# An attention and bilinear-GLU block: the condition and beta arrive as rows, one block of the modulation weights is loaded ahead of x, half of segment 1's row statistics move among the gates, and the first fifteen slots are filled evenly

## The chip, the cores and the metric

One core of a Trainium2 chip runs the whole program. The metric is the device time of one execution in microseconds (us). The kernel before has a median of 853.55 us over three runs (853.47 to 854.69).

## What is computed

`x` has 2048 rows of 512 columns. A condition vector `c` (512 numbers) gives six modulation vectors. The block is an adaptive layer norm, an attention over four segments of 512 rows with a memory carried from segment to segment, and a bilinear GLU. `_layernorm` subtracts the mean of a row and divides by the root of its variance plus 1e-5; `_silu(c)` is c / (1 + exp(-c)).

```python
x = A_x
mod = (_silu(c) @ w_mod).reshape(c.shape[0], 6, 1, -1)
sa, ca, ga, sb, cb, gb = (mod[:, i] for i in range(6))
h = _layernorm(x) * (1 + ca) + sa
x = x + ga * attention(h, wq, wk, wv, wo, beta)
h = _layernorm(x) * (1 + cb) + sb
x = x + gb * (((h @ w_gate) * (h @ w_up)) @ w_down)

# attention: H = 32 heads of 16, N = 4 segments of 512 rows, g = sigmoid(beta) for each head
for s in range(4):
    p = softmax(q_s k_s^T / 4 + mask)        # within the segment
    a_dot = p v_s
    a_mem = phi(q_s) M / (phi(q_s) z + 1e-6)  # phi(t) = t + 1 for t > 0, else exp(t)
    o_s = g * a_mem + (1 - g) * a_dot
    M, z = M + phi(k_s)^T v_s, z + sum(phi(k_s))
return o @ wo
```

The inputs are fp32. The kernel splits fp32 operands into a high and a low part (names that end in H and L) and adds three products.

## The kernel before, in words

The work on TensorE is kept in one written order: each matmul goes through a helper (`MM` and `TP`, L85 and L88) that chains it to the matmul before. Many VectorE and ScalarE instructions of the opening go through such chains too (`CV` and `CA`, L39). The scheduler places other instructions between them; `pin` ties one behind the last TensorE instruction. DMAs of weights and of `x` are issued by the SP queue, in its own order; two small ones by ScalarE's queue.

**The opening.** `s_c` is silu(c), kept as 128 partitions x 4 columns, so that each column scales one block of 128 rows of `w_mod`. `c` comes by a DMA straight into that layout; `beta` comes by a DMA that copies its 32 numbers to all 128 partitions (tile `be`). `xload(0)` issues the four 128x512 tiles of segment 0 of `x`; `wm0_load(j)` issues half j of the shift and scale columns of `w_mod` as four tiles `wm0_k` (k = 0 to 3, 256 KB each). `warm(NWU)` puts 18 matmuls on a tile of zeros (`wu` into `wups`) ahead of all other TensorE work. Then come

- `mod0(0)`: 16 fp32 matmuls (32 records of 128x96 in the profile, tile `m`) that multiply the first half of the columns with `s_c`,
- the 16 transposes of the normalised `x` (tile `atp`),
- `mod0(1)`: the second half. Its first two blocks are added up before, by ScalarE (`wm` scaled by `s_c`) and VectorE (scalar_tensor_tensor on `wm`), so 12 matmuls are left,
- the projections `kps`, `qps`, `vps` of segment 0, from `h` (tiles `ahH`, `ahL`).

VectorE takes the statistics of the four tiles of `x` (`bn_stats` and `bn_aggr`, tiles `ast`, `amv`) and normalises them in `ln`. `mod0_out` copies the modulation to `modc`, which ScalarE needs to build `ahf`.

**The gates.** `gates()` (about 27 to 37 us) makes `gg` = 1 + exp(-beta) and `omg` = 1 + exp(beta) and their reciprocals on VectorE; GpSimd puts `omg` into the `v` tiles and multiplies the masks `hmg`.

**The slots.** After that a loop over units `v` from -2 to 32 runs the attention, five slots a unit. A unit is four heads of one segment. In a slot, `q_half` runs q matmuls into bank `lq0` or `lq1` and a VectorE reduction that finds the row maximum (custom instruction, tiles `q` and `nm`); the bank is free for the next q matmul when the reduction is done. `k_step` runs the k matmuls into bank `lk`, ScalarE takes the exponential (tile `pt`). Between them `fill(share, ...)` takes steps from a generator of side work: it adds `share * 5.5` us of credit in each slot and spends it. The side work of segment 0 is the rest of the projections, the memory (`mp`, `mz`) and segment 1's layer norm (`a_ln(1)`), which the generator `weave` puts between the steps of the last q and k projections. In units -2, -1 and 0 there is no earlier unit to finish (`prev` is false); these are the first fifteen slots.

Of the kernel before, what the change touches and what calls it, by code (L numbers as in the profile page):

```python
# [8 lines left out]
F32 = mybir.dt.float32  # L9
# [8 lines left out]
P = 128  # L18
S, D, H, DH, NSEG, L, F = 2048, 512, 32, 16, 4, 512, 1376
KT = D // P  # L20
# [37 lines left out]
def tile_kernel(ctx, tc, x, wq, wk_, wv, wo, beta, w_gate, w_up, w_down, c, w_mod, out):  # L58
# [113 lines left out]
    def ln(pool, hpool, xt, s, sc, sh, pfx, hb, fast):  # L172
# [4 lines left out]
        for t in range(4):  # L177
            st = pool.tile([P, 6], F32, tag="st", name=f"{pfx}st{s}_{t}", bufs=2)
            i = V.bn_stats(st, xt[t])
            if not first:  # L180
                pin(i)
            V.bn_aggr(mv[:, t, :], st)
            if not first:
                yield 0.0
        sd = pool.tile([P, 4], F32, tag="sd", name=f"{pfx}sd{s}", bufs=2)
# [439 lines left out]

    pwpool, pw = open_pool(name="pw", bufs=1, reuse_waits="tile")
    papool, pa = open_pool(name="pa", bufs=2, reuse_waits="tile")
    nc.scalar.dma_start(s_c, c)
    wm = w_mod.rearrange("(k p) n -> p k n", p=P)

    def load_mod(i):
# [7 lines left out]
    def xload(s):  # L639
# [4 lines left out]
            xt.append(a)  # L644
        return xt

    xts = {0: xload(0)}
    NWU = 18
    wu = pa.tile([P, 512], BF, tag="rl", name="wu", bufs=1)
    vec.memset(wu, 0.0)  # L650
    wups = psp.tile([P, 2, 512], F32, tag="lk", name="wups", bufs=1)
# [2 lines left out]
        for i in range(n):  # L654
            MM(wups[:, 0], wu[:, 0:P], wu, start=True, stop=True)

    warm(NWU)
    wm0 = []
    for k in range(KT):
        a = ap.tile([P, 2, 2, 256], F32, tag="pt", name=f"wm0_{k}", bufs=PT)  # L660
        wm0.append(a)

    def wm0_load(j):
        for k in range(KT):
            pin(nc.sync.dma_start(wm0[k][:, j], wm[:, k, :].rearrange("p (i c) -> p i c", c=D)[:, 0:2, 256 * j:256 * j + 256]))

    wm0_load(0)
    r0 = [[a[:, j].rearrange("p i c -> p (i c)") for a in wm0] for j in range(2)]
    nc.scalar.dma_start(be, beta[None, :].to_broadcast([P, H]))
    act.activation(e1, s_c, AF.Exp, scale=-1.0)  # L670
    CV.tensor_scalar_add(e1, e1, 1.0)
    CV.reciprocal(e1, e1)
    scl = CV.tensor_mul(s_c, s_c, e1)
    for a in kst:
        tc.add_manual_dep(nc.gpsimd.memset(a[96:98].rearrange("p h t -> p (h t)").bitcast(F32), ONES2).ins, scl.ins.name, SYNC, reason="order")

    def gates():

        CA.activation(gg, be, AF.Exp, scale=-1.0)
        act.activation(omg, be, AF.Exp)  # L680
        CV.tensor_scalar(omg, omg, 1e30, 1.0, op0=ALU.min, op1=ALU.add)
        for a in vt[0] + vt[1]:
            nc.gpsimd.tensor_copy(a[:, 0:H * VS].rearrange("p (h e) -> p h e", e=VS)[:, :, DH], omg)
        CV.tensor_scalar_add(gg, gg, 1.0)
        for tl in (gg, omg):
            CV.reciprocal(tl, tl)
        for g in range(NG):
            nc.gpsimd.tensor_mul(hmg[:, g, :, 0:DH], hmg[:, g, :, 0:DH],
                                 gg[:, g * HG:(g + 1) * HG].unsqueeze(2).to_broadcast([P, HG, DH]))
            nc.gpsimd.tensor_mul(hmg[:, g, :, DH], hmg[:, g, :, DH], omg[:, g * HG:(g + 1) * HG])  # L690
# [28 lines left out]
    def mod0(j, ks=range(KT)):  # L719
        ps = mp0[j].rearrange("p (i n) -> p i n", n=P)[:, :, 0:MW]  # L720
        for k in ks:
            f = s_c[:, k:k + 1].to_broadcast([P, MW]) if len(ks) == KT or k > 1 else ones[:, 0:MW]
            for i in range(4):
                MM(ps[:, i], r0[j][k][:, i * P:(i + 1) * P], f,
                   start=k == ks[0] and i == 0, stop=k == KT - 1, skip_group_check=True)

    hcur = [None]

# [13 lines left out]
                i += 1  # L742

    wH, wL = {}, {}
    stage = [("ph", 3), ("ph", 3), ("ph", 3), ("mem", 1), ("pkr", 1), ("f", 2)] + [("x", 4)] * 4 + [("mem", 1), ("memb", 2)]
    nst = [0]

    def staged(nm):
        tg, n = stage[nst[0] % len(stage)]
        nst[0] += 1  # L750
        return (ap if tg == "memb" else pa).tile([P, D], F32, tag=tg, name=f"wr{nm}", bufs=n)

    def load_g(nm, w, g):
# [223 lines left out]
    def fill_a():  # L977
# [1 line left out]
            next(w)  # L979
        yield from av  # L980
        memq.extend((a_mem(0, 0), a_mem(0, 1)))
        lns = None
        for s in range(NSEG):
            if s > 0:
                hcur[0] = yield from lns
# [2 lines left out]
            for g in range(2 if s == 0 else 0, NG):  # L988
# [693 lines left out]
```

## Time and profile before

| | |
|---|---|
| Median of three runs | 853.55 us |
| Profiled execution | 854.15 us |
| Its span in the profile | 852.4 us |
| PE busy | 835.3 us (98%) |
| DVE busy | 643.1 us (75%) |
| ACT busy | 499.0 us (59%) |
| POOL busy | 276.8 us (32%) |

PE is TensorE's matmuls, PEld its weight loads, DVE is VectorE, ACT is ScalarE, POOL is GpSimd. A row of the timeline has the start, the busy time, the engine, the line, the operation, output <- input and the count; brackets give the idle time before it and who ended it. In rows that sum up a stretch (its start and end, its length, then busy time of each engine with its count, the granted clock, the DMA share and GB/s) the busy times are to be held against the length of the stretch. A matmul's busy time is longer than its spacing from the next one, because matmuls overlap; spacing is taken from starts.

### The profile page before, as it was taken

Reading aid. Unit: us, or ns where it says so; the run is one execution under the profiler, and the core shown is the slowest. Engines: PE = TensorE matmul, PEld = TensorE weight load, DVE = VectorE, ACT = ScalarE, POOL = GpSimd, SP = SyncE. Lnnn points to the kernel's source line nnn. Section 1 sums busy time; section 2 is a strip of 40 time slices with the busy share of each in tenths; the row PEclk is TensorE's granted clock in tenths of the full one; section 3 lists DMA queues with packets and bytes.
Section 4 is the critical chain, followed back from the end, with each engine's and each line's share of the span. In section 5 each row is a group of like instructions: output and inputs, shape, how many; then the busy total and the mean of one; then the engine's idle time right before and its main releaser. Section 6 shows DMA issues by size and latency. Waiting matters only on the chain.

```text
span 852.4 us, 14404 instructions
## 1 busy us (share of the span) xinstructions
PE 835.3 (98%) x4972; PEld 597.4 (70%) x4972; DVE 643.1 (75%) x1797; ACT 499.0 (59%) x760; POOL 276.8 (32%) x423
## 2 busy tenths in 40 slices
PE   9989999999999999999999999999999999999998
PEld 6756656666665656666665687888888778888886
DVE  7897768887778967787888359989987855447654
ACT  4758767787676876677545626344435555555330
POOL 2756627566565774675434610000000000000000
PEclk9999999999999999999999999999999999999999
DMA  9645435563545554466675466587650685335102
GB/s 271 155 152 155 121 104 141 158 179 115 143 106 166 144 165 106 122 170 213 195 216 155 145 192 230 189 287 271 253 201 28 234 271 210 121 135 184 43 8 98
DMA packets 83928, 139.57 MB, mean 164 GB/s; under 512 B 12720, under 2 KB 46768, under 8 KB 83856
## 3 DMA queue, kind: packets, MB, share of 16 engines
q1 hardware_dynamic: 83424, 138.51, 52.0%
q8 instruction: 39, 0.64, 0.3%
q14 instruction: 33, 0.27, 0.1%
q10 hardware_dynamic: 432, 0.15, 0.1%
HBM read 89.87 MB, written 48.50 MB: 162 GB/s over the span
## 4 chain that ended last, share of the span: by engine, by line
PE 61%; DVE 5%; ACT 1%; issue 0%; POOL 0%; DVEq 0%
PE acc L1358 14%; PE Xg L1289 7%; PE Xu L1289 6%; PE wops L85 5%; PE tb L85 5%; PE Yu L1289 4%; PE Yg L1289 4%; PE k L85 3%; PE q L85 3%; DVE q L39 2%; PE Zg L1289 1%; PE Zu L1289 1%; PE qps L85 1%; PE vps L85 1%; PE Xx L1289 1%; PE up L85 1%
## 5 line engine op out<-in xcount | busy, mean ns | idle before, releaser
L39 DVE CUSTOM_DVE_ANT_0 q<-q,cmask 128x384 f32<-128x384 f32 (+3 forms) x512 | 248.2, 503 | 71.1 <-PE q L85 63.5
L335 ACT ACTIVATE pt<-k 128x1024 f32<-128x1024 f32 x160 | 164.0, 1025 | 74.2 <-PE k L85 71.4
L341 POOL TENSOR_SCALAR_AFFINE_SELECT pt<-pt 128x256 f32<-128x256 f32 (+1 forms) x224 | 98.0, 452 | 137.2 <-ACT pt L335 136.9
L85 PE MATMUL q<-kst,qst 96*128 96x384 bf16 (+3 forms) x512 | 122.8, 302 | 6.5 <-DVE nm L39 5.1
L85 PE MATMUL k<-qst,kst 98*128 98x384 bf16 (+3 forms) x512 | 96.0, 299 | 1.6 <-ACT pt L335 1.3
L1366 DVE TENSOR_TENSOR xa<-xa,acc 128x512 f32<-128x512 f32 x95 | 64.9, 684 | 39.6 <-PE acc L1358 37.8
L85 PEld LDWEIGHTS <-qst 96*128 96x128 bf16 x512 | 43.9, 98 | 58.4 <-issue 43.6
L85 PE MATMUL tb<-pt,v 128*32 128x512 f32 (+3 forms) x1024 | 75.5, 436 | 0.0
L39 DVE DVE_READ_ACCUMULATOR2_ANT nm<- 128x1 f32 x512 | 71.8, 140 | 0.0
L85 PEld LDWEIGHTS <-kst 98*128 98x128 bf16 x512 | 44.4, 98 | 24.9 <-issue 8.8
L1358 PE MATMUL acc<-dH,mH 128*128 128x512 f32 (+1 forms) x152 | 60.3, 397 | 0.0
L1358 PE MATMUL acc<-dL,mH 128*128 128x512 f32 (+1 forms) x152 | 60.1, 395 | 0.0
L1358 PE MATMUL acc<-dH,mL 128*128 128x512 f32 (+1 forms) x152 | 60.0, 395 | 0.0
L85 PEld LDWEIGHTS tb<-pt,v 128*32 128x32 f32 x1024 | 28.7, 109 | 38.6 <-issue 35.7
L367 ACT ACTIVATE tsb<-tb 128x512 f32<-128x512 f32 x32 | 19.1, 596 | 31.6 <-PE tb L85 31.5
L1358 PEld LDWEIGHTS acc<-dH,mL 128*128 128x128 f32 (+1 forms) x152 | 28.5, 188 | 7.1 <-DVE mL L1309 0.3
L1358 PEld LDWEIGHTS acc<-dL,mH 128*128 128x128 f32 (+1 forms) x152 | 28.6, 188 | 7.0
L1358 PEld LDWEIGHTS acc<-dH,mH 128*128 128x128 f32 (+1 forms) x152 | 28.5, 188 | 6.8
L85 PE MATMUL kps<-ahH,wkH 128*128 128x512 f32 x64 | 29.4, 460 | 0.0
L85 PE MATMUL qps<-ahH,wqH 128*128 128x512 f32 x64 | 28.7, 448 | 0.2 <-DVE oL L39 0.2
L85 PE MATMUL vps<-wvH,ahH 128*128 128x512 f32 x64 | 28.3, 442 | 0.0
L85 PE MATMUL wops<-woH,oH 128*128 128x512 f32 x64 | 28.3, 442 | 0.0
(403 smaller groups left out, 2019.1 us busy)
## 6 DMA issues: line engine op xcount, KB each, us to landing
wm<-in_w_mod_dram SPq DMA_DIRECT2D x24, 256.0 KB, 3.9
kd<-k SPq DMA_DIRECT2D x16, 384.0 KB, 2.5
qd<-q SPq DMA_DIRECT2D x16, 384.0 KB, 3.5
kst<-kd SPq DMA_DIRECT2D x32, 192.0 KB, 3.2
qst<-qd SPq DMA_DIRECT2D x32, 192.0 KB, 3.7
x<-in_x_dram SPq DMA_DIRECT2D x16, 256.0 KB, 4.8
kst<-kd SPq DMA_DIRECT2D x32, 128.0 KB, 3.2
qst<-qd SPq DMA_DIRECT2D x32, 128.0 KB, 3.7
```

The source lines that it names most:

```text
L39: i = getattr(self.eng, name)(*a, **k)
L85: return pe(nc.tensor.matmul(*a, **k))
L335: ex = act.activation(pt, kp, AF.Exp, scale=0.25)
L341: sels[u, i] = nc.gpsimd.affine_select(w, w, pattern=[[0, w.shape[1]], [1, P]], compare_op=ALU.is_ge, fill=0.0, base=0, channel_multiplier=-1)
L367: act.activation(tsbs[u], tbs.pop(u), AF.Copy)
L1289: pe(nc.tensor.matmul(ps[0:n], a, b[:, k], start=first and c == 0, stop=last and c == 5, skip_group_check=True))
L1358: pe(nc.tensor.matmul(ps, a[0:m, t * P:(t + 1) * P], b[0:m], start=j == 0, stop=j == n - 1))
L1366: vec.tensor_add(xa, xa, ps)
```

## The change

It does four things.

1. `c` is loaded as 4 rows of 128 numbers and `beta` as one row of 32, and two small TensorE matmuls (`cps`, `bps`) lay them out over the partitions: `crow` against the identity, and a column of ones against `brow`. ScalarE then takes the exponential from `cps` and copies `bps` to `be`. The last steps of `s_c` on VectorE (`condition()`) stand behind the statistics of the first tile of `x`.
2. SP issues the first of the four `wm0` tiles of half 0 ahead of the four tiles of `x`, the other three behind them. The 18 warm-up matmuls become 3, then `cps` and `bps`, then 2, then block 0 of `mod0(0)`, then 4, then blocks 1 to 3.
3. Segment 1's `x` is issued before the last weight loads of the opening, and the statistics of its first two tiles stand next to the two reciprocals in `gates()`. The third is taken in the slot of the q projection where the first two stood. Four staging buffers of the weights move from the `x` ring to the `pt` ring.
4. In units -2, -1 and 0 the share is 0.2 in each of the five slots, in place of 0.25, 0, 0.25, 0.25, 0.25.

```diff
@@ in ln
             V.bn_aggr(mv[:, t, :], st)
+            if first and t == 0:
+                condition()
@@
-    nc.scalar.dma_start(s_c, c)
+    crow = pa.tile([P, D], F32, tag="mem", name="crow", bufs=1)[0:KT, 0:P]
+    brow = pa.tile([P, D], F32, tag="pkr", name="brow", bufs=1)[0:1, 0:H]
+    nc.scalar.dma_start(crow, c)
+    nc.scalar.dma_start(brow, beta[None, :])
@@
-    xts = {0: xload(0)}
-    NWU = 18
...
-    warm(NWU)
...
-    wm0_load(0)
+    wm0_load(0, (0,))
+    xts = {0: xload(0)}
...
+    warm(3)
+    cps = pst((P, KT), "sm", "cps")
+    MM(cps, crow, ident[0:KT, 0:KT], start=True, stop=True)
+    bps = pst((P, H), "tb", "bps")
+    MM(bps, ones[0:1, :], brow, start=True, stop=True)
+    warm(2)
+    wm0_load(0, (1, 2, 3))
...
-    nc.scalar.dma_start(be, beta[None, :].to_broadcast([P, H]))
-    act.activation(e1, s_c, AF.Exp, scale=-1.0)
-    CV.tensor_scalar_add(e1, e1, 1.0)
-    CV.reciprocal(e1, e1)
-    scl = CV.tensor_mul(s_c, s_c, e1)
+    act.activation(e1, cps, AF.Exp, scale=-1.0)
+    act.activation(be, bps, AF.Copy)
+
+    def condition():
+        CV.tensor_scalar_add(e1, e1, 1.0)
+        CV.reciprocal(e1, e1)
+        scl = CV.tensor_mul(s_c, cps, e1)
...
@@ in gates
         CV.tensor_scalar_add(gg, gg, 1.0)
+        vec.eng = CV
         for tl in (gg, omg):
             CV.reciprocal(tl, tl)
+            next(ln1)
@@
-    stage = [...] + [("x", 4)] * 4 + [("mem", 1), ("memb", 2)]
+    stage = [...] + [("pt", PT)] * 4 + [("mem", 1), ("memb", 2)]
@@ in fill_a
-                        xts[s + 1] = xload(s + 1)
-                        lns = a_ln(s + 1)
-                        Q = weave(Q, lns, (0, 1, 2, 3))
+                        if s > 0:
+                            xts[s + 1] = xload(s + 1)
+                            lns = a_ln(s + 1)
+                        Q = weave(Q, lns, (0, 1, 2, 3) if s > 0 else (0, 3))
@@
-    mod0(0)
+    mod0(0, (0,))
+    warm(4)
+    mod0(0, (1, 2, 3))
...
+    xts[1] = xload(1)
...
+    ln1 = a_ln(1)
     gates()
@@
-    share = (0.25, 0.0, 0.25, 0.25, 0.25)
...
+        share = (0.25, 0.0, 0.25, 0.25, 0.25) if prev else (0.2,) * 5
```

On TensorE, at the very start, the order before ends its warm-up and goes on in one piece (`wu` and `wups` are the warm-up, `m` the modulation, `atp` the transposed `x`):

```order
L85 LDWEIGHTS wu
L85 MATMUL wups<-wu 128x512
L85 MATMUL m_248<-s_c,wm_0_231 128x96 x4
L85 MATMUL m_248<-s_c,wm_1_232 128x96 x4
L85 MATMUL m_248<-s_c,wm_2_233 128x96 x4
L85 MATMUL m_248<-s_c,wm_3_234 128x96 x4
L88 MATMUL atp_0_318<-ident,x_0_202 128x128
```

The order now has the two layout matmuls after the third warm-up matmul, and four warm-up matmuls between block 0 and block 1 of the modulation:

```order
L85 MATMUL wups<-wu 128x512
L85 MATMUL cps<-ident,crow 128x4
L85 MATMUL bps<-brow,ones 128x32
L85 LDWEIGHTS wu
L85 MATMUL wups<-wu 128x512
...
L85 MATMUL m_235<-s_c,wm_0_205 128x96 x4
L85 LDWEIGHTS wu
L85 MATMUL wups<-wu 128x512
...
L85 MATMUL m_235<-s_c,wm_1_206 128x96 x4
L85 MATMUL m_235<-s_c,wm_2_207 128x96 x4
L85 MATMUL m_235<-s_c,wm_3_208 128x96 x4
L88 MATMUL atp_0_316<-ident,x_0_210 128x128
```

So TensorE can reach block 0 only when `s_c` is there, and `s_c` now needs a TensorE matmul, ScalarE and the first tile of `x`.

On VectorE the gates stand like this before (`omg` and `gg` are the gates, `phk_1` the feature map of k, `q_0_0` the first reduction of the slots):

```order
L39 TENSOR_SCALAR omg<-omg 128x32
L39 TENSOR_SCALAR gg<-gg 128x32
L39 RECIPROCAL gg<-gg 128x32
L39 RECIPROCAL omg<-omg 128x32
L853 SCALAR_TENSOR_TENSOR phk_1_539<-phk_1_539,rlk_1_540 128x512
L39 ISA q_0_0_590,nm_589<-q_0_0_590,cmask 128x512
```

And like this now:

```order
L39 RECIPROCAL gg<-gg 128x32
L39 BN_STATS ast_0_510<-x_0_433 128x6
L39 BN_AGGR amv_509<-ast_0_510 128x2
L39 RECIPROCAL omg<-omg 128x32
L39 BN_STATS ast_1_514<-x_1_435 128x6
L39 BN_AGGR amv_509<-ast_1_514 128x2
L39 SCALAR_TENSOR_TENSOR phk_1_552<-phk_1_552,rlk_1_553 128x512
```

Two pairs of statistics have moved in, one behind each reciprocal.

Still on VectorE, in unit -1 (rows of the second unit's reductions `q_2_0` to `q_3_1`), the place they came from reads before:

```order
L39 ISA q_2_0_743,nm_683<-q_2_0_743,cmask 128x512
...
L39 BN_STATS ast_0_747<-x_0_635 128x6
L39 BN_AGGR amv_746<-ast_0_747 128x2
L39 BN_STATS ast_1_753<-x_1_637 128x6
L39 BN_AGGR amv_746<-ast_1_753 128x2
L39 ISA q_2_1_759,nm_683<-q_2_1_759,cmask 128x512
...
L39 SCALAR_TENSOR_TENSOR phk_2_723<-phk_2_723,rlk_2_724 128x512
L39 ISA q_3_0_763,nm_683<-q_3_0_763,cmask 128x384
...
L39 BN_STATS ast_2_775<-x_2_639 128x6
L39 BN_AGGR amv_746<-ast_2_775 128x2
L39 ISA q_3_1_787,nm_683<-q_3_1_787,cmask 128x384
```

and now:

```order
L39 ISA q_2_0_748,nm_688<-q_2_0_748,cmask 128x512
...
L39 BN_STATS ast_2_751<-x_2_437 128x6
L39 BN_AGGR amv_509<-ast_2_751 128x2
L39 ISA q_2_1_760,nm_688<-q_2_1_760,cmask 128x512
...
L39 SCALAR_TENSOR_TENSOR phk_2_728<-phk_2_728,rlk_2_729 128x512
L39 ISA q_3_0_764,nm_688<-q_3_0_764,cmask 128x384
...
L39 ISA q_3_1_776,nm_688<-q_3_1_776,cmask 128x384
```

The third pair has moved up to where the first two stood, and nothing stands between `q_3_0` and `q_3_1`. On TensorE, in the same place, three `qps` matmuls go from before `q_3_1` to behind `mz_1`. Behind segment 0 the orders of all engines are the same as before.

More of the change, by code (lines that the diff above doesn't have):

```diff
@@ L645, in xload, with wm0_load @@
         return xt
+    wm0 = []
+    for k in range(KT):
+        a = ap.tile([P, 2, 2, 256], F32, tag="pt", name=f"wm0_{k}", bufs=PT)
+        wm0.append(a)
+    def wm0_load(j, ks=range(KT)):
+        for k in ks:
+            pin(nc.sync.dma_start(wm0[k][:, j], wm[:, k, :].rearrange("p (i c) -> p i c", c=D)[:, 0:2, 256 * j:256 * j + 256]))
+    wm0_load(0, (0,))
     xts = {0: xload(0)}
-    NWU = 18
     wu = pa.tile([P, 512], BF, tag="rl", name="wu", bufs=1)
@@ L655, in warm @@
             MM(wups[:, 0], wu[:, 0:P], wu, start=True, stop=True)
-    warm(NWU)
[L658 to L665, printed above, removed]
-    wm0_load(0)
-    r0 = [[a[:, j].rearrange("p i c -> p (i c)") for a in wm0] for j in range(2)]
-    nc.scalar.dma_start(be, beta[None, :].to_broadcast([P, H]))
-    act.activation(e1, s_c, AF.Exp, scale=-1.0)
-    CV.tensor_scalar_add(e1, e1, 1.0)
-    CV.reciprocal(e1, e1)
-    scl = CV.tensor_mul(s_c, s_c, e1)
-    for a in kst:
-        tc.add_manual_dep(nc.gpsimd.memset(a[96:98].rearrange("p h t -> p (h t)").bitcast(F32), ONES2).ins, scl.ins.name, SYNC, reason="order")
+    warm(3)
[5 more added lines that the diff above has]
+    wm0_load(0, (1, 2, 3))
+    r0 = [[a[:, j].rearrange("p i c -> p (i c)") for a in wm0] for j in range(2)]
+    act.activation(e1, cps, AF.Exp, scale=-1.0)
[4 more added lines that the diff above has]
+        scl = CV.tensor_mul(s_c, cps, e1)
+        for a in kst:
+            tc.add_manual_dep(nc.gpsimd.memset(a[96:98].rearrange("p h t -> p (h t)").bitcast(F32), ONES2).ins, scl.ins.name, SYNC, reason="order")
     def gates():
@@ L721, in mod0 @@
         for k in ks:
-            f = s_c[:, k:k + 1].to_broadcast([P, MW]) if len(ks) == KT or k > 1 else ones[:, 0:MW]
+            f = s_c[:, k:k + 1].to_broadcast([P, MW]) if j == 0 or k > 1 else ones[:, 0:MW]
             for i in range(4):
                 MM(ps[:, i], r0[j][k][:, i * P:(i + 1) * P], f,
-                   start=k == ks[0] and i == 0, stop=k == KT - 1, skip_group_check=True)
+                   start=k == j and i == 0, stop=k == KT - 1, skip_group_check=True)
     hcur = [None]
@@ L744, in tile_kernel @@
     wH, wL = {}, {}
-    stage = [("ph", 3), ("ph", 3), ("ph", 3), ("mem", 1), ("pkr", 1), ("f", 2)] + [("x", 4)] * 4 + [("mem", 1), ("memb", 2)]
+    stage = [("ph", 3), ("ph", 3), ("ph", 3), ("mem", 1), ("pkr", 1), ("f", 2)] + [("pt", PT)] * 4 + [("mem", 1), ("memb", 2)]
     nst = [0]
@@ L750, in staged @@
         nst[0] += 1
+        if tg == "pt":
+            return ap.tile([P, 2, 512], F32, tag=tg, name=f"wr{nm}", bufs=n)[:, 0]
         return (ap if tg == "memb" else pa).tile([P, D], F32, tag=tg, name=f"wr{nm}", bufs=n)
@@ L981, in fill_a @@
         memq.extend((a_mem(0, 0), a_mem(0, 1)))
-        lns = None
+        lns = ln1
         for s in range(NSEG):
@@ L1669 @@
     vals[0] = vals[0].reshape(S, D)
-    vals[9] = vals[9].reshape(KT, P).T
+    vals[9] = vals[9].reshape(KT, P)
     nc = _bacc.Bacc("TRN2", target_bir_lowering=False, num_devices=1, dynamic_dma_scratch_size=1024)
```

## The prediction

> **What bounds the kernel now.** I read the busy time by stretches first. Columns are the stretch, its length, busy time of each engine, the granted clock, the DMA share and GB/s.
>
> ```profile
> 8.76:16.94 8.18, 8.15 (x72) 7.99 (x72) 6.25 (x16) 4.83 (x8) 0.00 (x0) 1.00 1.10 345
> ...
> 44.00:60.00 16.00, 13.31 (x78) 9.05 (x77) 15.50 (x60) 10.07 (x15) 8.76 (x8) 1.00 0.54 167
> 60.00:76.00 16.00, 15.74 (x116) 10.33 (x115) 14.30 (x54) 11.89 (x19) 7.38 (x17) 1.00 0.29 81
> 76.00:845.00 769.00, 760.69 (x4560) 544.51 (x4559) 576.29 (x1605) 451.23 (x687) 239.88 (x356) 1.00 0.51 163
> ```
>
> PE is the first busy column: it has no gap behind 8.76 us and hardly any behind 60. In between, from 44 to 60 us, it is idle for 16.00 - 13.31 = 2.69 us, and there DVE (the third) is busy 15.50 of 16.00. So time can be won in two places: before 8.76, by bringing PE's unbroken work forward, and between 44 and 60, by taking work off DVE. Past 76 us the change alters no order, and PE's load is 98.9%, so what is won or lost by then should be carried to the end.
>
> The opening on PE, from its timeline, and the spacing of the warm-up from the weight loads:
>
> ```profile
> 1.69 6.82 PE L85 MATMUL wups<-wu 128*128 128x512 bf16 x18 [1.69 <-DVE wu L650]
> 8.79 3.78 PE L85 MATMUL m<-s_c,wm 128*128 128x96 f32 x32 [0.27 <-DVE ast L39]
> 12.41 1.91 PE L88 MATMUL atp<-ident,x 128*128 128x128 f32 x16
> 14.27 1.13 PE L85 MATMUL m<-ones,wm 128*128 128x96 f32 x8
> 15.24 1.95 PE L85 MATMUL m<-s_c,wm 128*128 128x96 f32 x16
> 16.97 0.48 PE L85 MATMUL kps<-ahH,wkH 128*128 128x512 f32 x1
> ```
>
> ```profile
> 6.79 0.15 PEld L85 LDWEIGHTS <-wu 128*128 128x128 bf16 x1 [0.28 <-issue]
> 7.21 0.80 PEld L85 LDWEIGHTS <-wu 128*128 128x128 bf16 x4 [0.28 <-issue]
> ```
>
> The warm-up matmuls are 7.21 - 6.79 = 0.42 us apart up to 7.2 us, then four loads fit in 0.80, which is 0.22 apart. PE runs at half rate from 1.69 to about 7.2, 5.5 us of unbroken matmuls, and at full rate from there. (The granted clock reads 1.00 in the stretch rows; the spacing tells more here.) All modulation, transposes and projections run at full rate, back to back.
>
> **Part 1, the DMAs of the opening.** The stretch in which `beta` is loaded and the one behind it, and the issue of `be` with its size and its time to landing:
>
> ```profile
> 3.25:5.75 2.50, 2.50 (x7) 0.91 (x6) 1.30 (x5) 0.20 (x1) 1.11 (x2) 1.00 0.37 112
> 5.75:9.50 3.75, 3.48 (x15) 1.64 (x14) 2.51 (x6) 0.71 (x3) 2.51 (x3) 1.00 1.07 375
> ```
>
> ```profile
> be<-in_beta_dram ACTq DMA_DIRECT2D x1, 16.0 KB, 5.2
> ```
>
> For 2.5 us the rate is 112 GB/s, then 375, while the 16 KB of `be`, one row copied 128 times, takes 5.2 us to land. I read `be` as the cause. With one row in its place the loads come 2.50 x (1 - 112/375) = 1.75 us earlier; if the dip has another cause, 0. All loads of the opening have the same total size, so the last `wm` block lands earlier too, and the DMAs stop being what PE waits for.
>
> **Part 2, when s_c is ready.** DVE's chain of the opening:
>
> ```profile
> 3.94 0.17 DVE L39 TENSOR_SCALAR e<-e 128x4 f32<-128x4 f32 x1 [1.16 <-ACT e L670]
> 4.14 0.18 DVE L39 RECIPROCAL e<-e 128x4 f32<-128x4 f32 x1
> 4.35 0.16 DVE L39 TENSOR_TENSOR s_c<-s_c,e 128x4 f32<-128x4 f32 x1
> 4.43 0.69 DVE L39 BATCH_NORM_STATS2 ast<-x 128x6 f32<-128x512 f32 x1
> 5.16 0.18 DVE L39 BATCH_NORM_AGGREGATE amv<-ast 128x2 f32<-128x6 f32 x1
> ...
> 8.77 0.18 DVE L39 BATCH_NORM_AGGREGATE amv<-ast 128x2 f32<-128x6 f32 x1
> ...
> 10.35 1.91 DVE L39 TENSOR_SCALAR x<-x,amv,ay 128x512 f32<-128x512 f32 x4
> ...
> 13.46 0.75 DVE L39 SCALAR_TENSOR_TENSOR wm<-wm,s_c,wm 128x512 f32<-128x512 f32 x1 [0.63 <-DMA wm<-in_w_mod_dram]
> ```
>
> ```profile
> 0.82 1.81 SPq L643 DMA_DIRECT2D x<-in_x_dram  x4
> ...
> DMA to landing us min/median/max: 2.7/5.0/5.7
> ```
>
> Now the first DMA of SP is `wm_0`, landing as `x_0` does before, at 0.82 + 2.7 = 3.5; `x_0` is 256 KB behind it, 0.70 us at 375 GB/s, so 4.2. Statistics and aggregate take 4.43 to 5.34, 0.91 us, then the three steps of `s_c` 3.94 to 4.51, 0.57: `s_c` is ready at 5.7, against 4.51. `cps`, `bps` and the two ACT steps are new, but end before that: `c` has landed and passed ACT by 3.94 before, `crow` should land no later, and one PE step more of about 0.3 us (an estimate, below the 0.48 of the wide `kps` above) ends at 4.3. Queued behind this wait on DVE are the other statistics: three pairs of 0.90 from 5.7 end at 8.4, against 8.77 + 0.18 = 8.95; normalising, which ends at 10.35 + 1.91 = 12.26 before, so ends at 11.7. The kst memsets of POOL wait for `s_c` too and have nobody behind them.
>
> **Part 3, PE from 5.7 us, and the term I am least sure of.** PE has only five warm-up matmuls of 0.42 and two small ones before 5.7 (about 1.69 to 2.95, then some 0.85 us from 3.7), and idles for about a microsecond ahead of block 0. From 5.7 it has work without a break: block 0 is 8 records at 3.62/32 = 0.113, 0.90 us; four warm-ups 0.88; 24 records 2.72: together 4.50 at full rate, 9.0 at half. If full rate begins at time T, `mod0(0)` ends at 5.7 + 4.50 + (T - 5.7)/2 = 10.2 + (T - 5.7)/2. The trace gives two bounds for T. If what counts is the time since the first matmul, T = 7.2 and the end is 10.95. If 5.5 us of unbroken work are needed as before, T = 5.7 + 5.5 = 11.2 and the end is 12.95. Before it is 12.41, so the opening gains 1.46 or loses 0.54. The gain is capped at 1.3: `x` is normalised only at 11.7, and the second half waits for the DVE step at 13.46, whose DMA comes at most 1.75 earlier. I take the middle of the two ends, 11.95, since the early matmuls are broken but not absent: a gain of 0.46, taken as **0.4**, with bounds of 1.3 won and 0.5 lost.
>
> Here a rule of the skill speaks against the change. The Trainium skill, "TensorE: Matmul & The Clock Gate", Part 1 (the warmup mystery), says that the clock is halved until one busy window of about 3.4 us is over, and that the windows run free of the kernel's start. By that rule a window busy throughout can begin no sooner than 5.7, T is 9.1 to 12.5, and the end 11.9 to 13.6, so the opening would gain 0.5 or lose 1.2, on the whole a loss of 0.35.
>
> **Part 4, the slots.** DVE in the stretch that it bounds, and what PE waits for there:
>
> ```profile
> L39 DVE BATCH_NORM_STATS2 ast<-x x4: 660/688/690, 51.2 to 59.2; 128x6 f32<-128x512 f32 x4
> ```
>
> ```profile
> 53.59 0.38 PE L85 MATMUL q<-kst,qst 96*128 96x384 bf16 x2 [0.43 <-DVE nm L39]
> 53.80 0.60 PE L85 MATMUL k<-qst,kst 98*128 98x512 bf16 x2
> 55.06 0.38 PE L85 MATMUL q<-kst,qst 96*128 96x256 bf16 x2 [0.66 <-DVE nm L39]
> 55.28 1.09 PE L85 MATMUL mz<-v,pkr 128*128 128x136 f32 x8
> 56.73 0.38 PE L85 MATMUL q<-kst,qst 96*128 96x256 bf16 x2 [0.36 <-DVE nm L39]
> ```
>
> Two pairs leave it: 2 x (0.69 + 0.18) = 1.74 us of DVE. PE's waits for DVE right behind them are 0.43 + 0.66 + 0.36 = 1.45. The gain can't be over 1.74 by DVE and not over 2.69 by PE's idle time of the stretch; the even shares, which put three `kps` and three `qps` matmuls where PE waits, allow a little more than the pairs alone. What is late next is ACT's exponential and PE itself, at 98% behind 60 us. I take **1.4**, nearest the row of waits; bounds 0 and 2.0.
>
> The pairs go to where DVE is idle:
>
> ```profile
> 30.92 0.35 DVE L39 RECIPROCAL gg<-gg 128x32 f32<-128x32 f32 x1
> 32.20 0.35 DVE L39 RECIPROCAL omg<-omg 128x32 f32<-128x32 f32 x1 [0.92 <-POOL v L683]
> 33.57 3.80 DVE L853 SCALAR_TENSOR_TENSOR phk<-phk,rlk 128x512 f32<-128x512 f32 x1 [1.02 <-ACT phk L848]
> 37.30 0.69 DVE L39 CUSTOM_DVE_ANT_0 q<-q,cmask 128x512 f32<-128x512 f32 x1
> ```
>
> 0.92 + 1.02 = 1.94 us of idle time covers 1.74, so I cost it at nothing. If POOL slows them as it slows `phk` there (3.80 against 0.75 for the same operation in the opening), `phk` starts later but also meets less of POOL's work; cost 0 to 0.3. The loads of segment 1's `x`, four of 256 KB or 2.8 us at 375 GB/s, go in front of two weight loads and the first kd and qd on SP. They can start when the transposes of segment 0 are done, about 14, and have flowed by about 20; kd waits for the k projection, whose last matmuls follow the first `kps` of 16.97 by several us. Cost nothing.
>
> **The sum.** 0.4 + 1.4 = 1.8. The profiled execution took 854.15 (span 852.4 and 1.75 around it), so it would be 852.35. It lies 0.60 above the median of 853.55; from the median, **851.75**.
>
> **The rivals.**
> - Full rate comes early. PE's first matmuls count in spite of the breaks, T = 7.2 and the opening gains its 1.3: 853.55 - 1.3 - 1.4 = 850.85. For it speaks that breaks are about a microsecond each; against it that PE's unbroken matmuls from 1.69 to 6.8 did not suffice before.
> - Full rate comes late, as the unbroken 5.5 us suggest: the opening loses 0.5, the slots win 1.4, 852.65. The whole gain on the DMAs is then lost to PE's clock. (The Trainium skill's "TensorE: Matmul & The Clock Gate", Part 1, makes this the likely course, with 0.35 in place of 0.5.)
> - Slower: the 96-column records with their long weight loads (PEld 7.99 of 8.18 us) do not count as work that raises the clock, so half rate lasts through `mod0(0)` (to 14.7), the transposes (to 18.4). With T = 18 and 4.50 + 1.86 + 2.70 = 9.06 us of work up to the first `kps`, that starts at 5.7 + 9.06 + 6.15 = 20.9, against 16.97: 3.9 lost, 1.4 won, 856.05. It decides from T = 12.9, where the opening loses the 1.4. Against it: before, these records kept full rate.
> - The slots give nothing: ACT or PE takes the place of DVE, 853.15.
>
> **How the numbers follow.** A measurement of this kernel can tell about 0.2%, 1.7 us, from no change. Forecast 0.44, its own range 850.6 to 852.9, 0.27 of it faster by more than 1.7 and 0.17 not; early 0.23, faster; late 0.16, same; half rate through the transposes 0.11, slower; nothing from the slots 0.06, same. Faster 0.50, same 0.39, slower 0.11. The range takes in both parts' bounds, -1.3 - 2.0 and +0.5 + 0, with 0.3 for the spread of the runs: 849.9 to 854.4. Only the slower rival lies outside.
>
> **What would show it.** Right: GB/s near 375 from 3.3 us on, first `m` at 5.7 to 6.0, `atp` at about 12.0, first `kps` at 16.5; from 44 to 60 us the same PE records in 1.4 us less, and `phk` at the gates still ending near 37 minus the opening's gain. Wrong: a dip in GB/s that stays, `m` records 0.2 apart past 11 us, a first `kps` behind 17.5, or waits of PE for `pt` where those for `nm` were.

## The result, and the profile after

The changed kernel takes **857.52 us** (median of six runs, 856.26 to 858.25), the kernel before 853.57 on the same chip (853.47 to 854.69): a ratio of 1.0042, with a 95% interval of 1.0031 to 1.0052. It is slower by 2.6 to 4.4 us, where 1.8 us of gain were forecast. (The medians are 3.95 us apart; the ratio takes in all runs and makes it 3.6.) The profiled execution took 857.53 us, with a span of 855.8. All six runs have a mean granted clock of 0.996 or 0.997; the runs of the kernel before that stand beside the experiments have 0.999 or 1.000.

Up to 62 us the forecast holds almost to the tenth in the profiled execution. The opening, from PE's timeline of the changed kernel:

```profile
5.76 2.02 PE L85 MATMUL m<-s_c,wm 128*128 128x96 f32 x8 [0.31 <-DVE s_c L39]
7.58 1.91 PE L85 MATMUL wups<-wu 128*128 128x512 bf16 x4
9.28 3.13 PE L85 MATMUL m<-s_c,wm 128*128 128x96 f32 x24
12.25 1.91 PE L88 MATMUL atp<-ident,x 128*128 128x128 f32 x16
16.59 0.47 PE L85 MATMUL kps<-ahH,wkH 128*128 128x512 f32 x1
```

The first `m` stands at 5.76, the first `kps` at 16.59 against 16.97. The stretches behind the opening (length, busy PE, PEld, DVE, ACT, POOL, granted clock, DMA share, GB/s):

```profile
44.00:60.00 16.00, 14.72 (x86) 9.89 (x85) 15.18 (x60) 10.95 (x17) 8.20 (x10) 1.00 0.29 78
60.00:76.00 16.00, 12.88 (x80) 7.49 (x79) 9.58 (x32) 7.78 (x11) 5.99 (x12) 0.79 0.36 101
```

From 44 to 60 us PE is busy 14.72 where it was busy 13.31: the slots gain what was promised. From 60 to 76 us it is busy 12.88 where it was 15.74, and the granted clock has a mean of 0.79, where before it was 1.00. ACT's rows date the turn. `kf` is ACT's copy of a finished k projection, `tsb` its copy of the first finished attention tile. The `kf` of group 3 and the first `tsb` before:

```profile
63.25 0.60 ACT L820 ACTIVATE kf<-kps 128x512 f32<-128x512 f32 x1 [0.19 <-PE kps L85]
69.43 0.60 ACT L367 ACTIVATE tsb<-tb 128x512 f32<-128x512 f32 x1 [0.59 <-PE tb L85]
```

and after:

```profile
61.43 0.60 ACT L837 ACTIVATE kf<-kps 128x512 f32<-128x512 f32 x1
73.53 0.60 ACT L369 ACTIVATE tsb<-tb 128x512 f32<-128x512 f32 x1 [1.95 <-PE tb L85]
```

The changed kernel is 63.25 - 61.43 = 1.82 us ahead at `kf` and 73.53 - 69.43 = 4.10 us behind at `tsb`: 5.9 us are lost in 12. (The profiled executions end 857.53 - 854.15 = 3.4 apart. Of the 0.7 that came back, 0.5 did so near 518 us, where PE's wait for `mL` is 0.34 us in place of 0.60.)

What happens there is read backward from PE. PE of the changed kernel:

```profile
61.69 0.40 PE L85 MATMUL qps<-ahL,wqH 128*128 128x512 f32 x1
65.22 0.58 PE L85 MATMUL q<-kst,qst 96*128 96x512 bf16 x1 [3.12 <-DVE nm L39]
```

PE waits 3.12 us for a row maximum of DVE, that is, for a bank that DVE has yet to read. DVE:

```profile
60.12 0.14 DVE L39 DVE_READ_ACCUMULATOR2_ANT nm<- 128x1 f32 x1
62.89 1.35 DVE L39 TENSOR_SCALAR x<-x,amv,ay 128x512 f32<-128x512 f32 x1 [2.63 <-POOL ay L201]
64.16 0.55 DVE L39 CUSTOM_DVE_ANT_0 q<-q,cmask 128x384 f32<-128x384 f32 x1
```

DVE isn't busy. It stands 2.63 us at the normalising of segment 1's `x`, which waits for `ay` from POOL, and the row maximum that PE needs is behind it in DVE's queue. POOL:

```profile
59.12 0.20 POOL L198 TENSOR_SCALAR ayb<-amv 128x4 f32<-128x4 f32 x1
59.36 0.77 POOL L343 TENSOR_SCALAR_AFFINE_SELECT pt<-pt 128x256 f32<-128x256 f32 x2
60.10 1.16 POOL L846 TENSOR_TENSOR q<-qr,q 128x512 bf16<-128x512 f32 x1
61.22 0.20 POOL L194 TENSOR_TENSOR aya<-ay 128x4 f32<-128x4 f32 x1
61.49 0.20 POOL L199 TENSOR_TENSOR ayb<-ayb,aya 128x4 f32<-128x4 f32 x1
61.64 0.77 POOL L343 TENSOR_SCALAR_AFFINE_SELECT pt<-pt 128x256 f32<-128x256 f32 x2
62.38 0.19 POOL L200 TENSOR_SCALAR ayb<-ayb 128x4 f32<-128x4 f32 x1
62.65 0.20 POOL L201 TENSOR_TENSOR ay<-ay,ayb 128x4 f32<-128x4 f32 x1
```

Five steps of 0.2 us take from 59.12 to 62.85, because 1.16 us of a q conversion and twice 0.77 us of selects stand between them. Before, the same place on POOL and DVE reads:

```profile
60.16 0.19 POOL L196 TENSOR_SCALAR ayb<-amv 128x4 f32<-128x4 f32 x1 [1.07 <-DVE amv L39]
60.66 0.77 POOL L341 TENSOR_SCALAR_AFFINE_SELECT pt<-pt 128x256 f32<-128x256 f32 x2 [0.31 <-ACT pt L335]
61.40 0.20 POOL L192 TENSOR_TENSOR aya<-ay 128x4 f32<-128x4 f32 x1
62.25 0.20 POOL L199 TENSOR_TENSOR ay<-ay,ayb 128x4 f32<-128x4 f32 x1
```

```profile
62.48 0.55 DVE L39 TENSOR_SCALAR x<-x,amv,ay 128x512 f32<-128x512 f32 x1 [0.40 <-POOL ay L199]
```

There the chain takes 2.3 us, with one 0.77 of selects in it, and DVE waits 0.40. The even shares move the end of group 2's q projection to a later slot (its last three `qps` start at 54.60 us in place of 52.22), so its conversion, which POOL began at 56.94 before, arrives at 60.10, in the middle of the chain.

The wait is the first half of the loss. The rest is the clock. Its record changes in steps of 3.41 us: full rate from 9.93, half rate from 64.54, which is 54.61 or 16 steps later, full rate again from 71.37. Stretches cut at these steps around the wait, in the changed kernel:

```profile
61.13:64.54 3.41, 0.96 (x5) 0.54 (x4) 1.65 (x2) 2.08 (x4) 2.66 (x8) 1.00 0.81 233
64.54:67.95 3.41, 2.73 (x12) 2.02 (x12) 3.10 (x12) 1.33 (x3) 1.32 (x2) 0.50 0.83 227
67.95:71.37 3.42, 3.42 (x13) 1.37 (x16) 2.61 (x10) 2.10 (x4) 0.47 (x1) 0.50 0.02 7
71.37:74.78 3.41, 3.41 (x43) 2.01 (x36) 0.76 (x5) 0.81 (x2) 0.41 (x1) 1.00 0.02 5
```

Behind the stretch in which PE is busy 0.96 of 3.41, the granted clock is 0.50 for two such stretches. PE's 2.73 + 3.42 = 6.15 us of work in them would take half as long at full rate: 3.1 us. With the wait of 3.1 that is 6.2, near the 5.9 lost.

### The profile page after: what moved, and what is told of

Same layout as the page of the kernel before. It is cut to its first block, busy times and chain, and to the rows that moved or that the text cites. A ratio compares the mean times of both kernels' runs of the same rounds, so it can differ in the third digit from the quotient of the medians.

```text
span 855.8 us, 14401 instructions
## 1 busy us (share of the span) xinstructions
PE 836.9 (98%) x4967; PEld 599.4 (70%) x4967; DVE 644.3 (75%) x1797; ACT 499.4 (58%) x761; POOL 275.5 (32%) x423
## 4 chain that ended last, share of the span: by engine, by line
PE 59%; DVE 5%; ACT 2%; issue 1%; DMA 1%; POOL 0%; SPq 0%; DVEq 0%; ACTq 0%
PE acc L1380 14%; PE Xu L1311 6%; PE Xg L1311 6%; PE wops L85 5%; PE tb L85 5%; PE Yu L1311 4%; PE Yg L1311 4%; PE k L85 3%; PE q L85 3%; DVE q L39 2%; PE Zg L1311 1%; PE Zu L1311 1%; PE qps L85 1%; PE vps L85 1%; PE Xx L1311 1%
## 5 line engine op out<-in xcount | busy, mean ns | idle before, releaser
L85 PEld LDWEIGHTS <-kst 98*128 98x128 bf16 x512 | 44.7, 98 | 28.3 <-issue 12.5
```

Source lines behind the costliest of these rows:

```text
L85: return pe(nc.tensor.matmul(*a, **k))
```

## The experiments

Theory A: the even shares empty PE, at 62 us by way of POOL's queue, and a nearly empty stretch halves the clock. A spell is a time of half rate. Its rivals: the moved statistics do it; the clock falls for another reason; the even shares cost by their order alone. Five rounds each; each run stands beside runs of the kernel before on the same chip, whose medians were 853.45 to 853.85 us.

**The shares of before** (changed kernel otherwise).

```diff
-        share = (0.25, 0.0, 0.25, 0.25, 0.25) if prev else (0.2,) * 5
+        share = (0.25, 0.0, 0.25, 0.25, 0.25)
```

> The changed kernel with the shares of before in all slots; opening and moved statistics stay. Theory A (POOL's queue, then the clock): the even shares put the last step of segment 2's... of group 2's q conversion (1.16 us) ahead of the small steps of segment 1's ay on POOL; DVE's normalising of x waits 2.63 us for ay, PE waits 3.12 us behind that, and this gap halves the granted clock from 64.5 to 71.4 us. Then here: DVE's wait for ay under 0.8 us, no PE wait over 1 us near 60 us, granted clock 1.00 throughout, 852.0 to 852.8 us (opening 0.4 and 0.4 to 1.2 of the two pairs won). Rival B (the moved statistics and the earlier x do it, by another timing of segment 1): wait and half rate stay, 856 to 858 us. Rival C (the opening shifts the phase of the clock's control, the wait is a bystander): half rate stays near 64 us although the wait is gone, about 854.5 us.

853.13 us (852.70 to 853.39), ratio 0.9990 (0.9981 to 1.0000). The spell of half rate and the long wait are gone, by DVE's timeline and by the stretch that was empty:

```profile
61.04 0.55 DVE L39 TENSOR_SCALAR x<-x,amv,ay 128x512 f32<-128x512 f32 x1 [0.65 <-POOL ay L201]
```

```profile
61.10:64.50 3.40, 3.05 (x19) 2.12 (x17) 3.37 (x9) 2.56 (x5) 1.95 (x3) 1.00 0.62 147
```

So B and C fall. The gain of the rest of the change is below A's figure, 0.0 to 1.6 us.

**The even shares alone** (the kernel before, the one line of the shares added).

> The kernel before with the even shares in the first fifteen slots alone. Theory A (the even shares empty PE at two places, and an empty stretch of about 3.4 us halves the clock): PE waits of 1 us or more near 53 or 64 us, a spell of granted clock 0.5 of 3.4 or 6.8 us behind one of them, 855 to 857 us. Rival (the harm needs the moved statistics as well): no spell, 853.2 to 854.2 us.

858.91 us (855.21 to 860.03), ratio 1.0054 (1.0037 to 1.0070): the whole loss, and more than A's 855 to 857. The three slowest runs, from 859.35, have a mean granted clock of 0.995 or 0.996, the fastest 0.999. In the profile the clock falls twice:

```profile
51.36:54.77 3.41, 1.57 (x12) 0.92 (x11) 3.31 (x12) 1.92 (x3) 1.47 (x1) 1.00 0.76 167
54.77:58.19 3.42, 3.42 (x15) 2.74 (x14) 2.58 (x11) 0.26 (x2) 0.41 (x1) 0.50 0.34 115
...
65.02:68.43 3.41, 0.61 (x5) 0.45 (x5) 2.98 (x8) 0.93 (x2) 2.65 (x4) 1.00 0.95 256
68.43:71.84 3.41, 3.41 (x14) 2.23 (x13) 2.92 (x9) 2.55 (x4) 0.65 (x2) 0.50 0.50 151
```

The second spell is that of the changed kernel: DVE waits 2.50 us for `ay` until 65.42. The first has another cause: near 53 us PE waits for DVE,

```profile
53.10 0.38 PE L85 MATMUL q<-kst,qst 96*128 96x384 bf16 x2 [1.18 <-DVE nm L39]
54.57 0.43 PE L85 MATMUL q<-kst,qst 96*128 96x256 bf16 x2 [0.66 <-DVE nm L39]
```

where before three `qps` matmuls (from 52.22 us) stood in that wait and 0.43 us of it was left. The even shares take them away.

**The statistics alone** (the kernel before, with two of the four statistics at the gates, the early `x`, and the staging buffers that this needs).

> The kernel before with two of segment 1's four statistics at the gates and its x loaded ahead of them (with the staging buffers that this needs), opening and shares as before. The prediction's term of 1.4 us for the slots rested on DVE's two pairs: if they are worth PE's waits for nm, 852.2 to 852.9 us; if PE's and ACT's order set the pace there, 853.4 to 853.9 us. Clock 1.00 throughout in both.

852.93 us (852.53 to 853.75), ratio 0.9993 (0.9985 to 1.0002). The upper end of the first figure; a gain of 0.9 by the medians, not to be told from none by the interval.

**The opening alone.**

> The kernel before with the new opening alone. Theory O1 (its full rate begins at 9.9 us as in the first profile, first kps at 16.6): 0.4 us less than before, 853.1 to 853.6, with runs within 0.4 us of each other. Theory O2 (full rate needs one window of 3.41 us that is busy throughout, and the windows run free of the kernel's start; the first such window can begin at 5.7 us at the soonest): full rate from anywhere in 9.1 to 12.5 us, first kps from 16.2 to 17.9 us, mean time 0 to 0.4 us above before, runs spread over 1.5 us.

854.19 us (852.92 to 854.82), ratio 1.0002 (0.9993 to 1.0010). O2's times hold and nothing is gained. (The spread of 1.9 us is no sign: the runs of the kernel before spread over 2.5 us on the same chip.) In its profile full rate begins at 10.74 us:

```profile
9.27 3.52 PE L85 MATMUL m<-s_c,wm 128*128 128x96 f32 x24
...
16.97 0.48 PE L85 MATMUL kps<-ahH,wkH 128*128 128x512 f32 x1
```

The first `kps` stands where it stood before. The 24 records of `m` take 3.13 us in the changed kernel, whose record of the clock has full rate from 9.93, and 3.52 here: the run decides.

**All statistics back in the slots** (changed kernel, even shares and opening stay).

> The changed kernel with segment 1's loads of x and all four statistics back in the slots; opening and even shares stay. Theory A by the order on POOL: here the q conversion's last step stands ahead of the chain's first step and nothing but two selects stands inside it, so wait and half rate go although the shares are even, 852.5 to 853.5 us. Rival B: the same, since the statistics are back. Rival D (even shares by themselves leave PE short of work at this place): wait of 2 us or more and half rate stay, 856 to 858 us.

855.38 us (853.93 to 856.38), ratio 1.0016 (1.0007 to 1.0025). Between the figures of A and D. Nothing but selects stands inside the chain here, and DVE still waits 1.85 us for `ay`: POOL's q conversion (61.34, 1.16 us) stands ahead of the chain, which begins at 62.59 though `amv` is there by 60.77. So a conversion ahead of the chain delays it as one inside it does. The spell in this profile is the early one:

```profile
51.03:54.44 3.41, 1.60 (x11) 0.89 (x10) 3.31 (x12) 1.70 (x3) 1.41 (x1) 1.00 0.75 190
54.44:57.86 3.42, 3.40 (x13) 2.80 (x12) 2.61 (x10) 0.42 (x1) 0.46 (x2) 0.50 0.34 115
...
64.68:68.10 3.42, 2.21 (x16) 1.56 (x14) 3.38 (x11) 1.93 (x4) 1.97 (x3) 1.00 0.91 206
```

The last row is worth keeping: with 2.21 of 3.41 busy the clock did not fall.

**PE kept awake in the late gap.**

```diff
                 for k, a, b in terms:
+                if (s, g, nm, n) == (0, 3, "q", 0):
+                    for _ in range(12):
+                        MM(ps, a[nm, g][:, k, :], b[k], start=True, stop=True)
                     MM(ps, a[nm, g][:, k, :], b[k], start=n == 0, stop=n == 11)
```

> The changed kernel; the first matmul of q's projection of group 3, which is PE's last work ahead of the 3.12 us wait, is issued 12 times more into the same bank (each with start, so the result is the same): 12 x 0.234 = 2.8 us of PE work that fits into the wait. Theory A (the empty stretch of PE lowers the clock): DVE's wait of 2.6 us stays, granted clock 1.00 throughout, and the loss of 6.83 x 0.5 = 3.4 us goes less PE's idle 0.5 of that time: 854.3 to 855.2 us. Rival E (the clock falls for another reason, for instance too much activity): 0.5 from about 64.5 us stays, 857 to 858 us.

855.82 us (854.99 to 856.57), ratio 1.0022 (1.0013 to 1.0031). The clock is 1.00 in the profile from the opening to the end of PE's work, 0.999 or 1.000 in the mean of each of the ten runs, and DVE's wait stays at 2.64 us. More work for PE takes the spell away and the kernel is 1.7 us faster by the medians, so E falls. The time is 0.6 above A's figure; since no run has a spell, the early gap isn't the reason by way of the clock, and the 0.6 stays open.

**PE kept awake in both gaps**: the same, and four transposes issued four times over.

```diff
-            for t in range(4):
+            for t in range(16 if (s, g) == (0, 1) else 4):
+                t %= 4
                 TP(mp[:, t * P:(t + 1) * P], ph["k"][:, t * P:(t + 1) * P], ident)
```

> The changed kernel with both gaps of PE filled by work whose result is thrown over: the first matmul of q's projection of group 3 12 times more (near 62 us), and the four transposes of mp of group 1 four times over (near 52 us). DVE's 2.6 us wait for ay stays. Theory A: no spell of half rate in the slots in any run, so what is left of the changed kernel's loss is the wait: 855.0 to 855.8 us, with runs closer together than with one gap filled. Rival (the gap near 52 us never mattered in the changed kernel): 855.8 us or more, as with one gap filled, since the transposes then delay the slots.

854.81 us (854.04 to 855.26), ratio 1.0013 (1.0004 to 1.0022), 0.2 below A's range, runs within 1.2 us, the mean granted clock 1.000 in all eleven. DVE still waits 2.65 us for `ay`, and the stretch around that wait is full:

```profile
62.77:66.18 3.41, 3.19 (x14) 2.36 (x13) 2.16 (x6) 1.59 (x3) 2.60 (x7) 1.00 0.96 264
```

PE does nothing useful in that wait and loses the time all the same, but the clock stays. From 1.0042 to 1.0013 is 0.0029, or 2.5 us of the changed kernel's 3.6; to 1.0022, with the late gap alone filled, it is 0.0020, or 1.7 us. Neither run has a spell, so what lies between the two isn't the clock, and the clock's part is an estimate of 1.7 to 2.5 us (each ratio is uncertain by 0.0009 to 0.0011). From 1.0013 down to the 0.9990 of the run with the shares of before 0.0023 is left, or 2.0 us, which is not the clock; most likely it is the wait.

**The chain early**: `ay` of segment 1 one fill step earlier (changed kernel otherwise).

```diff
-Q = weave(Q, lns, (0, 1, 2, 3) if s > 0 else (0, 3))
+Q = weave(Q, lns, (0, 1, 2, 3) if s > 0 else (0, 1, 3))
-K = weave(K, lns, (1,) if s > 0 else (0, 1, 3))
+K = weave(K, lns, (1,) if s > 0 else (1, 3))
```

> The changed kernel; the step that computes ay of segment 1 is taken one fill step earlier (last step of q's projection of group 2 in place of the first of k's of group 3), all else the same. On POOL its five small steps then stand ahead of the q conversion and of all selects. Theory A: DVE's wait for ay under 0.3 us, clock 1.00 throughout, all of the 5.7 us won back: 851.5 to 852.2 us. Rival C or D: half rate stays, 854 to 858 us.

853.96 us (852.63 to 855.01), ratio 1.0001 (0.9993 to 1.0010). The late wait is gone and 3.5 us with it, but not all: in the profile the early gap takes its place.

```profile
51.52:54.93 3.41, 1.58 (x12) 0.92 (x11) 3.31 (x12) 2.32 (x5) 1.80 (x3) 1.00 0.77 172
```

The granted clock is 0.50 in the 3.41 us behind it.

**The chain early and the early gap filled** with the repeated transposes.

> The run with ay of segment 1 computed one fill step earlier (853.96 us, granted clock 0.5 from 54.93 for 3.41 us), and the four transposes of mp of group 1, PE's last work ahead of the 1.17 us wait near 52 us, issued four times over into the same bank (same result): 12 x 0.09 = 1.1 us of PE work in that wait. Theory A (a window of 3.41 us in which PE is busy less than about half halves the clock): granted clock 1.00 throughout, the spell's loss of 3.41 x 0.5 = 1.7 us less 0.4 to 0.7 us of idle time in it goes: 852.5 to 853.1 us, runs closer together. Rival (PE's fill does not matter, the even shares cost by their order alone): 853.8 to 854.2 us.

853.74 us (853.20 to 854.76), ratio 1.0001 (0.9993 to 1.0010). Clock 1.00 throughout and the runs closer together, but no time won that could be told: the rival's figure within 0.1. The repeated transposes pass the wait on,

```profile
55.73 0.38 PE L85 MATMUL q<-kst,qst 96*128 96x256 bf16 x2 [1.54 <-DVE nm L39]
```

where 0.66 us stood. What the clock costs at the early gap can be read from runs of one kernel. With the chain early, eight runs have a mean granted clock of 0.997 or 0.998 and take 854.34 us on the mean, the three with 0.999 or 1.000 take 852.87: 1.5 us less. With all statistics in the slots, five runs with 0.997 or 0.998 take 856.00, the six with 1.000 take 854.80: 1.2 us less. So the spell has a price there too, about 1.2 to 1.5 us by these few runs (their openings differ as well), and the repeated transposes cost about what they save.

**Two more warm-up matmuls** with the shares of before: `warm(1)` between `cps` and `bps`, `warm(3)` in place of `warm(2)`.

> The changed kernel with the shares of before (as in the run without the even shares), and two more warm-up matmuls: one between condition's and beta's small matmul, one ahead of the first modulation block, so that PE has no gap of over 0.2 us from 1.7 us on. Theory O2: full rate between 5.1 and 8.6 us, the first half of the modulation ends near 11.7 us (x and the last wm block then set it), first kps at 15.7 to 16.2: 0.6 to 1.3 us less than without the two matmuls, 851.8 to 852.6 us, runs closer together. Theory O1 (small matmuls never count, only time since 5.7 us): full rate at 9.5 or later, 853.1 to 853.5 us.

852.44 us (851.26 to 854.46), ratio 0.9986 (0.9977 to 0.9995). The time is that of O2, the profile isn't: full rate from 10.62 in the profiled execution, though the rows show no gap of PE. The 3.41 us from 3.79 to 7.21 are full by their records, and no full rate follows. They hold `bps`, a matmul of one row and 32 columns whose pair of records lasts 0.6 us: it looks busy and may count as a gap. The next four runs move `bps`.

**`bps` and `be` behind the first modulation block**, `warm(5)` ahead of it, `warm(3)` behind it, shares of before.

> The changed kernel with the shares of before; beta's small matmul and its copy on ACT move behind the first modulation block, and five warm-up matmuls instead of two stand between condition's small matmul and that block (three instead of four behind it). Theory O2 (full rate needs one free-running window of 3.41 us that is all but full): windows that begin after 3.6 us are full, so full rate begins between 7.0 and 10.4 us, on the mean 1.8 earlier than the 10.5 of the runs so far, 0.3 to 0.9 us less than the 853.13 us with the shares of before alone: 852.2 to 852.8 us. Rival O3 (x and the last wm block set the end of the first modulation half anyway): 853.0 to 853.4 us.

851.97 us (851.33 to 854.08), ratio 0.9984 (0.9975 to 0.9993). That is 0.2 below O2's range, yet three runs in eleven stand above 853.4, among them the profiled one, with full rate from 11.69 only. There the stretch from 4.86 to 8.28 is full again and holds `bps`.

**The same with the chain early.**

> As the run with beta's matmul behind the first modulation block, and with ay of segment 1 computed one fill step earlier, which takes DVE's wait of 0.65 us for ay near 61 us away. If that wait is on the path: 0.3 to 0.6 us less than the run without it, 851.7 to 852.4 us; if PE's order sets the pace there: the same within 0.2 us.

851.73 us (851.13 to 854.62), ratio 0.9982 (0.9970 to 0.9994). The difference of 0.2 from the run without it is too small to settle.

**`bps` and `be` behind the whole first half** of the modulation, `warm(4)` again.

> As the run with beta's matmul behind the first modulation block and ay of segment 1 one fill step earlier, but beta's small matmul and its copy stand behind the whole first half of the modulation, with four warm-up matmuls after block 0 again. Theory O2 (the small matmul's record of 0.6 us is a light stretch that spoils a window): from 3.6 us on PE has no light stretch, so full rate begins between 7.0 and 10.4 us in every run, where the run with beta behind block 0 began it at 7.17 in one profile and its sister at 11.69: median 851.2 to 851.8 us, and no run above 853 us unless a spell falls in the slots. Rival (where beta's matmul stands does not matter): full rate past 10.5 us in some runs, median 851.7 us and the same spread of 3.5 us. It is also the version meant to beat both kernels.

852.26 us (851.24 to 852.84), ratio 0.9984 (0.9975 to 0.9993). No run is above 853, as O2 has it, but the median misses. Full rate from 4.99 in the profile is earlier than O2's 7.0: the stretch ahead of it, from 1.58, holds `cps` and is busy 3.30 of 3.41, and that sufficed. A new wait took the gain:

```profile
12.48 1.97 PE L88 MATMUL atp<-ident,x 128*128 128x128 f32 x16 [0.74 <-ACT be L1128]
```

`bps` held a PSUM bank of the transposes until ACT had copied it, behind a row that waits for `wm`.

**The same, `bps` in the free half of the warm-up's bank.**

```diff
-    bps = pst((P, H), "tb", "bps")
+    bps = wups[:, 1, 0:H]
```

> As the run with beta's small matmul behind the whole first half of the modulation, but its result goes to the free half of the warm-up's PSUM bank, so that no transpose waits for ACT's copy of beta. Theory O2: full rate between 5.0 and 10.4 us, transposes of x begin at 11.2 to 12.2 us, first kps at 15.8 to 16.6, median 851.2 to 851.8 us. Rival (x's normalising and the last wm block set the start of the second half, not PE's clock): first kps at 16.6 to 16.9 in spite of early full rate, 852.0 to 852.4 us.

**851.30 us** (850.98 to 851.98), ratio 0.9973 (0.9962 to 0.9984): 1.4 to 3.2 us faster than before, and faster than the changed kernel. This is the version that beats both.

```profile
16.21 0.48 PE L85 MATMUL kps<-ahH,wkH 128*128 128x512 f32 x1
```

## Why the prediction was wrong

- **Part 1** was right about the dip and too large in its price. In the stretch of the dip the changed kernel has 296 GB/s instead of 112,

```profile
3.25:5.75 2.50, 2.01 (x6) 0.95 (x6) 1.27 (x5) 0.60 (x3) 0.00 (x0) 1.00 0.95 296
```

but ACT's first step that waits for `wm` begins at 11.79 instead of 12.58: 0.79 us earlier, where 1.75 were forecast. That `be` made the dip isn't shown: the load of `c` changed with it in every run.
- **Part 2** was right for `s_c`: the wait for it ends at 5.76, forecast 5.7 to 6.0. It was wrong for the normalising of `x`, which ends at 12.35 where 11.7 was forecast, because DVE waits 0.82 us for the second tile of `x` until 6.53.
- **Part 3** was right for the profiled execution (0.38 for 0.4) and wrong for the median: the opening alone has a ratio of 1.0002. That the profiled execution agreed was luck, since its full rate began nearly the earliest of eight. The step of this part that failed is "I take the middle of the two ends" for T, as if T were one number. With this opening full rate began at 9.89, 9.93, 10.07, 10.55, 10.67, 10.74, 11.54 and 11.57 us in eight profiles, nearer the late end of 11.2. The rule of the Trainium skill ("TensorE: Matmul & The Clock Gate", Part 1), that a busy window of about 3.4 us must pass and that the windows run free of the kernel's start, gave an estimate of 9.1 to 12.5 us for T, and all eight lie in it.
- **Part 4**, the term of the statistics, had the right mechanism and came out at 0.9 us, by the medians of the run with the statistics alone, for 1.4. In the stretch where it was costed, 1.6 us were won: in the run with the shares of before, the `q` matmul that starts at 51.41 us before is 0.13 us ahead, the one at 57.64 is 1.70 ahead. The one at 66.69 is 0.73 ahead, so 1.0 us is lost again behind that stretch. DVE's wait for `ay` is 0.25 us longer there (0.65 for 0.40), and the normalising of the next tile of `x` takes 0.77 us longer; POOL's conversion now starts just ahead of it. DVE and POOL before:

```profile
64.46 0.54 DVE L39 TENSOR_SCALAR x<-x,amv,ay 128x512 f32<-128x512 f32 x1
64.59 1.43 POOL L825 TENSOR_TENSOR kr<-kf,k 128x512 f32<-128x512 f32 x1 [0.69 <-ACT k L824]
```

and with the shares of before in the changed kernel:

```profile
63.02 1.31 DVE L39 TENSOR_SCALAR x<-x,amv,ay 128x512 f32<-128x512 f32 x1
62.89 1.16 POOL L842 TENSOR_TENSOR kr<-kf,k 128x512 f32<-128x512 f32 x1 [0.68 <-ACT k L841]
```

The cover of the statistics at the gates held; nothing was lost there.
- **The step that failed** is the half sentence on the even shares, which "allow a little more than the pairs alone", with ACT and PE named as next late. I costed them by the gaps of PE that they could fill from 44 to 60 us, and not by the conversion of q that they move on POOL, nor by the gap from which they take the `qps` matmuls. The wait of 0.40 us for `ay` at 62.48 was in the trace of before, behind the stretch that I read. It was 2.63 after, and what was late next was POOL; PE's wait of 3.12 us behind it and the half rate from 64.54 to 71.37 turned the gain of 1.8 us into a loss.
- **The sum's last assumption**, that past 76 us nothing moves, held well enough: 4.1 us behind at 73.5, 3.4 at the end. **The rivals** had the clock as the slower case, but in the opening, through the 96-column records. It fell in the slots instead, behind a wait; none of the four had that.

## What to carry to other kernels

When side work is spread more evenly over slots, follow every queue that it passes: a small chain on a side engine that an in-order engine waits for costs what is put in its middle or ahead of it, and the work that leaves a wait uncovers it. A wait of TensorE can be dearer than its length: here a stretch of 3.41 us in which it was less than half busy was paid for a second time at half rate. Useless matmuls in an unavoidable wait can be worth their place; they were in the late gap and not in the early one. A gain in the opening that depends on when full rate begins is to be costed as a range over runs, not as one number.

## What the runs showed of the hardware

- The granted clock falls without PE being idle for long: in the early spell of the even shares alone the waits were 1.18 and 0.66 us. Stretches with 0.61, 0.96, 1.57, 1.58 and 1.60 us of PE in 3.41 were followed by half rate, stretches with 2.21 and 2.37 (the changed kernel's own, near 52 us) were not, and neither was the kernel before's last one with PE's work, 1.68 from 847.00 us. So the line lies close to half. The Trainium skill ("TensorE: Matmul & The Clock Gate", Part 1) gives an idle window of about 3.4 us as the condition; here windows that were 18 to 47% busy were enough, so the measurement differs from the page.

```profile
50.89:54.30 3.41, 2.37 (x18) 1.65 (x17) 3.31 (x14) 2.13 (x3) 1.39 (x2) 1.00 0.82 189
```

- Half rate lasted 3.41 us where the stretch behind the gap was 3.40 to 3.42 busy, and 6.83 where it was 2.73: coming back takes a fuller stretch than staying. In the openings 3.30 sufficed once; 2.92 in the changed kernel, from 3.10, did not.
- `bps` in an otherwise busy stretch kept full rate away. From 4.74 to 8.15 in the last run (warm-ups, block 0, warm-ups) PE is busy throughout and full rate follows; from 4.86 to 8.28 with `bps` behind block 0 it is busy throughout by the records as well, and full rate does not follow, nor behind 3.79 to 7.21 with two more warm-ups. `cps`, with 4 rows, did no such harm in the stretch of 3.30. That is one or two profiles each.
- A normalising of a 128x512 tile on VectorE that starts 0.01 to 0.13 us behind a conversion on POOL took 1.31 to 1.43 us in six profiles; one that starts 0.13 or 0.19 ahead of such a conversion took 0.54 in three, and POOL's conversion then took 1.38 to 1.43 in place of 1.16. Whichever came second was the slower one.
